# A bias row copied by another engine, and loads and scalings of q and k put elsewhere in their queues

## The chip, the core and the metric

The kernel runs on one core of a Trainium2 chip. A core has TensorE (PE in the profile, its weight loads PEld), VectorE (DVE), ScalarE (ACT), GpSimd (POOL) and SyncE (SP), which here only issues DMAs. Each engine works through its own instructions in the order in which they were written; an instruction that waits holds all that stands behind it on its engine, its DMA issues too. The metric is the device time of one execution in microseconds (us).

## What is computed

Eight batches with 12 heads of 448 tokens and 64 columns. q and k are normalized by their root mean square, attention follows, and its output, laid side by side over the heads (768 columns), goes through a gated layer whose one half is mixed over the tokens by `w_spatial`.

```python
q_n, k_n = rmsnorm(q, g_q), rmsnorm(k, g_k)      # x / sqrt(mean(x*x) + 1e-6) * g
scores = q_n @ k_n.transpose(0, 1, 3, 2) / sqrt(64)
attn = exp(scores - max); attn = attn / (sum(attn) + 1e-9)
x = (attn @ v) laid out as (batch, token, head * 64)
h = maximum(x @ w_in, 0); u, v = h[..., :512], h[..., 512:]
v_n = (v - mean(v)) / sqrt(var(v) + 1e-6)
v_s = einsum('ts,bsd->btd', w_spatial, v_n) + b_spatial[None, :, None]
out = (u * v_s) @ w_out
```

All inputs and the output are float32; the kernel multiplies in bfloat16.

## The kernel before

The 96 heads go in 24 **groups** of four heads, three groups to a batch; group 6 is the first of batch 2. For each group q and k have to be prepared: both are squared (`squares`, line 250, tile sqt; on GpSimd apart from the first ones), the squares are summed (`reduce`, line 258, tile ms, VectorE), the reciprocal root is made of the sums in two small activations (`rstd`, lines 266 and 267, tiles ln and rs, ScalarE), and q and k are multiplied by it (`scaled`, line 277, tile n; on GpSimd from group 4 on). Then a DMA issued by SyncE transposes them (`transpose_dma`, line 341, tiles qT and kr), and for k VectorE multiplies by the product of the two weight vectors (`k_scale`, line 347, tile kT). For groups 0 to 3 TensorE transposes instead.

The scores of a group are made in seven **passes** of two heads' pairs (line 367, or 363 for the pass with the odd tokens). The first 20 passes go one by one (`early`). From then on two passes make a **step**, numbered 10 to 83: eight score matmuls, then `rstd` of a group if the table puts one there, then one exponential of 128 x 1792 on ScalarE (line 374, tile et), then the rest of the table's work for this step, then either the attention output of a finished group (`attend`, lines 396 to 411: sums of the exponentials and their product with v, tile vt) or pieces of the gated layer (`fill`). Group G has its first scores at step 7G/2, rounded down.

Four things set the order of the work around the change, all written by hand. The table `todo` holds, by step, the parts of a group's preparation: `EVEN` and `ODD` give them relative to the step of the group's first scores ("sq" squares of q or k, "red" both sums, "rstd", "sc" scaling of q or k, "ks" `k_scale`), and `at` puts the transposition ("tr") one step behind each scaling. The loads of a later batch's q and k (`load_part`, four parts each, 128 rows of six heads at most; tiles qb and kb) are in the same table as "ld", from step 10 for batch 2, two parts a step. `v_step` puts the four loads of a later batch's v (`load_v`, line 130, issued by GpSimd) into steps; for batch 1 these are 10 to 13. And `load(1, 1, pool)` issues the four loads of group 1's k (lines 90 to 93, tile kf) from GpSimd at the very start.

The weights come in the first passes: `load_w_in` behind passes 3 and 8, `load_w_sp` (the spatial weights, and the bias row bst) behind pass 15, `load_w_out` at step 18. The gated layer of a batch is queued as small units (`gated`): v half (line 468), its statistics (476, 477), normalization on GpSimd (486, 490), u half (498), the mixing over the tokens (508), the output (527), its copy (443 or 445) and its store by SyncE (535 to 538). For batch 0 the queue also holds `bias_row` and four `w_sp_unit`: these bring the spatial weights, transposed by TensorE and copied by VectorE (line 223), into the tile w_spT, whose partition 64 holds the bias in its last block. The bias row is one partition of 448 values; `bias_row` writes it in three pieces, with steps of 4 or 3 elements on the reading side (lines 229 to 232).

## Time and profile before

| what | us |
|---|---|
| median of 3 runs | 344.07 |
| lowest and highest run | 343.49, 344.3 |
| profiled execution, whole | 340.97 |
| its span in the profile | 339.2 |

The profile is of one execution. Its page gives the busy time of each engine, the chain of work that ended last and the costliest groups of instructions; the trace behind it answers where an engine stood idle, for whom, and what stood in its queue then. "Idle before" is the time that an engine waited in front of an instruction, and the arrow names what ended the wait. DMA issues are shown with the engine that issues them (POOL, SPq); the time to landing is from the issue to the arrival of the data.

### The profile page before, as it was taken

The page shows a single profiled execution, that of the slowest core. Times are in us where ns is not written, and L with a number is a line of the kernel's source. Part 1 is how long each engine was busy: PE and PEld are TensorE (multiplying, and loading weights), DVE is VectorE, ACT ScalarE, POOL GpSimd, SP SyncE. Part 2 cuts the span into 40 slices and gives each one's busy share as a digit, 9 for nine tenths or more (in the row PEclk, how much of TensorE's full clock was granted, in tenths as well). Part 3 has the DMA queues.
Part 4 walks back from the last instruction along what each step waited for, and adds up shares of the span by engine and source line. Part 5 has one row for each costly group of instructions (what it writes and reads, how often), then busy time and mean ns, then how long its engine had stood idle before and what let it go on. Part 6 is the DMA issues. An engine that isn't in the chain of part 4 may idle for free.

```text
span 339.2 us, 6451 instructions
## 1 busy us (share of the span) xinstructions
PE 278.5 (82%) x2527; PEld 130.0 (38%) x2537; DVE 212.5 (63%) x343; ACT 211.2 (62%) x273; POOL 205.1 (60%) x183
## 2 busy tenths in 40 slices
PE   7587694790598799798688889779799979999994
PEld 7244331340243344244333344334334433444552
DVE  3876616499849467387467584495397486645652
ACT  2677766391157778567476778658477786675421
POOL 6759886689307499529908699359744993120210
PEclk9789978795589999989999999999799999999998
DMA  7999999829970999936992999857947387131145
GB/s 164 196 203 227 225 180 210 165 23 186 190 129 2 188 186 280 199 47 117 224 230 59 198 181 268 167 102 122 271 105 128 45 175 116 25 93 48 24 139 164
DMA packets 82944, 50.90 MB, mean 150 GB/s; under 512 B 46753, under 2 KB 79170, under 8 KB 82914
## 3 DMA queue, kind: packets, MB, share of 16 engines
q1 hardware_dynamic: 67218, 41.53, 59.1%
q0 software_dynamic: 15408, 8.73, 20.9%
q8 instruction: 20, 0.33, 0.4%
q10 hardware_dynamic: 288, 0.23, 0.2%
q14 instruction: 10, 0.08, 0.1%
HBM read 38.55 MB, written 11.01 MB: 146 GB/s over the span
## 4 chain that ended last, share of the span: by engine, by line
PE 27%; POOL 23%; DVE 15%; DMA 13%; issue 10%; ACT 6%; SPq 4%; POOLq 0%; DVEq 0%; ACTq 0%
POOL sqt L250 9%; DMA kr<-n 7%; PE ps L396 7%; POOL n L277 7%; DVE ms L258 5%; PE ps L527 4%; PE ps L508 4%; POOL vn L490 4%; PE ps L468 4%; PE ps L498 4%; ACT et L374 3%; DMA kf<-in_k_dram 3%; PE pss L367 3%; DVE s L476 3%; POOL vt L130 2%
## 5 line engine op out<-in xcount | busy, mean ns | idle before, releaser
L374 ACT ACTIVATE et<-pss 128x1792 bf16<-128x1792 f32 x74 | 122.9, 1661 | 68.5 <-PE pss L367 55.2
L411 DVE TENSOR_TENSOR xt<-ps,rc 128x448 bf16<-128x448 f32 x48 | 28.3, 621 | 62.2 <-ACT rc L404 43.5
L250 POOL TENSOR_TENSOR sqt<-kb 128x896 f32<-128x896 f32 x18 | 30.3, 1683 | 45.8 <-DVE ms L258 23.7
L367 PE MATMUL pss<-qT,kT 64*128 64x448 bf16 x254 | 38.1, 360 | 20.1 <-DVE kT L347 15.7
L396 PE MATMUL ps<-et,vt 128*32 128x448 bf16 x768 | 47.4, 385 | 7.9 <-DMA vt<-in_v_dram 5.7
L527 PE MATMUL ps<-w_out,gt 128*128 128x384 bf16 (+1 forms) x256 | 47.5, 327 | 3.0 <-DVE osb L445 2.2
L258 DVE TENSOR_REDUCE ms<-sqt 128x14 f32<-128x896 f32 x46 | 47.7, 1075 | 2.5 <-POOL sqt L250 2.5
L468 PE MATMUL ps<-w_in_v,xt 128*128 128x512 bf16 (+1 forms) x182 | 45.5, 381 | 0.4
L498 PE MATMUL ps<-xt,w_in_u 128*128 128x448 bf16 x192 | 40.3, 353 | 2.5 <-DVE osb L445 1.7
L347 DVE TENSOR_SCALAR_CACHE_REDUCE kT<-kr,g_col 128x896 bf16<-128x896 bf16 x20 | 22.7, 1136 | 26.3 <-DMA kr<-n 26.3
L396 PEld LDWEIGHTS <-vt 128*32 128x32 bf16 x768 | 23.1, 104 | 27.6 <-issue 16.2
L527 PEld LDWEIGHTS <-gt 128*128 128x128 bf16 (+1 forms) x256 | 24.2, 100 | 22.5 <-issue 9.3
L277 POOL TENSOR_TENSOR n<-qb,rs 128x896 bf16<-128x896 f32 x18 | 30.4, 1690 | 1.9 <-ACT rs L267 1.9
L367 PEld LDWEIGHTS <-kT 64*128 64x128 bf16 x276 | 10.5, 94 | 54.7 <-issue 30.9
L486 POOL TENSOR_SCALAR nm<-mv 128x4 f32<-128x4 f32 x8 | 1.8, 222 | 48.9 <-DVE mv L477 48.9
L277 POOL TENSOR_TENSOR n<-kb,rs 128x896 bf16<-128x896 f32 x18 | 30.4, 1689 | 0.1
L250 POOL TENSOR_TENSOR sqt<-qb 128x896 f32<-128x896 f32 x18 | 30.3, 1682 | 0.0
L445 DVE COPY osb<-ps 128x384 f32<-128x384 f32 (+1 forms) x45 | 24.4, 556 | 9.3 <-PE ps L527 7.9
L508 PE MATMUL ps<-w_spT,vn 128*128 128x448 bf16 (+1 forms) x128 | 28.8, 369 | 0.0
L490 POOL TENSOR_SCALAR vn<-vs,nm,rv 128x512 bf16<-128x512 bf16 (+1 forms) x32 | 24.0, 767 | 7.1 <-ACT rv L485 6.3
L498 PEld LDWEIGHTS <-w_in_u 128*128 128x128 bf16 x192 | 17.3, 98 | 21.6 <-issue 8.0
L468 PEld LDWEIGHTS <-xt 128*128 128x128 bf16 (+1 forms) x192 | 17.7, 100 | 19.8 <-issue 5.5
(94 smaller groups left out, 366.2 us busy)
## 6 DMA issues: line engine op xcount, KB each, us to landing
out_dram<-osb SPq DMA_DIRECT2D x55, 192.0 KB, 3.8
qb<-in_q_dram SPq DMA_DIRECT2D x12, 384.0 KB, 5.4
kb<-in_k_dram SPq DMA_DIRECT2D x12, 384.0 KB, 6.9
qb<-in_q_dram SPq DMA_DIRECT2D x12, 288.0 KB, 5.6
kb<-in_k_dram SPq DMA_DIRECT2D x12, 288.0 KB, 6.1
vt<-in_v_dram POOLq DMA_DIRECT2D x16, 192.0 KB, 5.1
vt<-in_v_dram POOLq DMA_DIRECT2D x16, 144.0 KB, 4.8
qf<-in_q_dram SPq DMA_DIRECT2D x10, 128.0 KB, 4.3
```

Source lines behind the costliest of these rows:

```text
L250: pool.tensor_tensor(out=t, in0=x, in1=x, op=ALU.mult)
L258: dve.tensor_reduce(out=sqs[gk][:, key[1], :], in_=sqt.pop(key).rearrange("p h c d -> p (h c) d"), axis=AX.X, op=ALU.add)
L277: (eng or pool).tensor_tensor(out=t.rearrange("p c h d -> p h c d"), in0=raw[key], in1=rst[gk][:, key[1], :].rearrange("p (h c) -> p h c", ...
L367: pe.matmul(out=ps[:, h, 0:S], lhsT=kT[r, c0:c0 + 128], rhs=qT[r, :], start=True, stop=True, tile_position=(64 * h, 0))
L374: act.activation(out=ets[s][:, 2 * a:2 * a + 2 * m, :], in_=ps[:, 0:2 * m, 0:S], func=AF.Exp, bias=0.0, scale=1.0)
L396: pe.matmul(out=ps[32 * l:32 * l + 32, 0:S], lhsT=w, rhs=et_of(G, 3 if r == 3 else r + 4 * y, h), start=(r == 0), stop=(r == 3), tile_posi ...
L411: dve.tensor_tensor(out=xts[b][:, 2 * g + half, :], in0=pst.pop((G, half))[:, 0:S], in1=rec[G], op=ALU.mult)
L468: pe.matmul(out=ps[0:m, :], lhsT=xts[b][:, j, t0:t0 + m], rhs=w_in_v[:, j, :], start=(j == 0), stop=(j == 5), tile_position=(0, 0))
L490: pool.tensor_scalar(out=vn_t[b % 2][0:m, c, :], in0=vs[b][c][0:m, :], scalar1=nms[b][0:m, c:c + 1], scalar2=rvs[b][0:m, c:c + 1], op0=ALU ...
L498: pe.matmul(out=ps[:, 0:S], lhsT=w_in_u[:, j, 128 * f:128 * f + 128], rhs=xts[b][:, j, :], start=(j == 0), stop=(j == 5))
L508: pe.matmul(out=ps[:, 0:S], lhsT=vn_t[b % 2][0:kp, c, 128 * f:128 * f + 128], rhs=w_spT[0:kp, c, :], start=(c == 0), stop=(c == NT - 1))
L527: pe.matmul(out=ps[o:o + m, 0:384], lhsT=gts[b][f][:, t0:t0 + m], rhs=w_out[:, f, r], start=(f == 0), stop=(f == 3), tile_position=(0, o))
```

## The change

The three copies of `bias_row` go from VectorE to ScalarE. The four loads of group 1's k are issued by GpSimd behind its first square and no longer ahead of it. The four loads of batch 1's v go together behind pass 15, ahead of the squares of group 4 and of the spatial weights. In the table, q of a group from 5 on is scaled in the step of its `rstd`, where it had a step of its own behind it, and k one step sooner than it was (group 5's k comes one step later); groups 6 and 7 are put one or two steps later than that, apart from `k_scale`. The loads of batch 2 begin at step 12 and not at 10.

```diff
--- before.py
+++ after.py
@@ -148,7 +148,6 @@
     g_row = const.tile([1, 2, 2, D], FP)
     pool.dma_start(out=g_row[:, 0], in_=bass.AP(tensor=g_q.tensor, offset=g_q.offset, ap=[[0, 1], [0, 2], [1, D]]))
     pool.dma_start(out=g_row[:, 1], in_=bass.AP(tensor=g_k.tensor, offset=g_k.offset, ap=[[0, 1], [0, 2], [1, D]]))
-    load(1, 1, pool)
     eps = const.tile([P, 1], FP)
     dve.memset(eps, 1e-6)
     one_f = const.tile([1, 1], FP)
@@ -226,10 +225,10 @@
         row = w_spT[64:65, NT - 1, :]
         b = bst[64:65, :]
         main = row[:, 0:384].rearrange("o (m r) -> o m r", r=P)
-        dve.tensor_copy(out=main[:, :, 0:64],
-                        in_=b[:, 0:256].rearrange("o (r m) -> o m r", m=4)[:, 0:3, :])
-        dve.tensor_copy(out=main[:, :, 64:128], in_=b[:, 256:S].rearrange("o (r m) -> o m r", m=3))
-        dve.tensor_copy(out=row[:, 384:S], in_=b[:, 3:256:4])
+        for o, i in ((main[:, :, 0:64], b[:, 0:256].rearrange("o (r m) -> o m r", m=4)[:, 0:3, :]),
+                     (main[:, :, 64:128], b[:, 256:S].rearrange("o (r m) -> o m r", m=3)),
+                     (row[:, 384:S], b[:, 3:256:4])):
+            act.activation(out=o, in_=i, func=AF.Copy, bias=0.0, scale=1.0)
 
 
     sqt, sqs, rst, nrm, qkt = {}, {}, {}, {}, {}
@@ -584,6 +583,7 @@
 
     squares(0, 0, 0, eng=act)
     squares(0, 1, 0)
+    load(1, 1, pool)
     reduce(0, 0, 0)
     reduce(0, 1, 0)
     squares(0, 0, 1, eng=act)
@@ -644,6 +644,7 @@
             rstd(3)
             scaled(3, 1)
             scaled(3, 0, eng=dve)
+            load_v(1, range(4))
             squares(4, 0)
             squares(4, 1)
             load_w_sp()
@@ -668,12 +669,14 @@
 
 
 
-    EVEN = {-8: ("sq", 0), -7: ("sq", 1), -6: ("red",), -5: ("rstd",), -4: ("sc", 0), -3: ("sc", 1), -1: ("ks",)}
-    ODD = {-6: ("sq", 0), -5: ("sq", 1), -4: ("red",), -3: ("rstd",), -2: ("sc", 0), -1: ("sc", 1), 2: ("ks",)}
+    EVEN = {-8: ("sq", 0), -7: ("sq", 1), -6: ("red",), -5: ("rstd",), -4: ("sc", 1), -1: ("ks",)}
+    ODD = {-6: ("sq", 0), -5: ("sq", 1), -4: ("red",), -3: ("rstd",), -2: ("sc", 1), 2: ("ks",)}
     todo = {}
 
     def at(s, G, *what):
         todo.setdefault(s, []).append((G,) + what)
+        if what[0] == "rstd" and G > 4:
+            at(s, G, "sc", 0)
         if what[0] == "sc":
             at(s + 1, G, "tr", what[1])
 
@@ -686,14 +689,13 @@
     at(12, 5, "sq", 1)
     at(13, 5, "red")
     at(14, 5, "rstd")
-    at(14, 5, "sc", 0)
-    at(14, 5, "sc", 1)
+    at(15, 5, "sc", 1)
     at(16, 5, "ks")
     for G in range(6, NGT):
         for o, what in (ODD if G % 2 else EVEN).items():
-            at(7 * (G // 2) + o, G, *what)
+            at(7 * (G // 2) + o + (2 if G < 8 and o < (-4, -2)[G % 2] else 1 if G < 8 and o < -1 else 0), G, *what)
     for b in range(2, B):
-        s0 = max(S0 if b == 2 else 17, NCH * NG * b // 2 - 17)
+        s0 = max(S0 + 2 if b == 2 else 17, NCH * NG * b // 2 - 17)
         for n in range(8):
             at(s0 + n // (2 if b < 4 else 1), NG * b, "ld", n)
 
@@ -721,7 +723,7 @@
         return (NCH * G + NCH - 1) // 2 + 1
 
     gate_step = {attend_step(NG * b + 2) + 1: b for b in range(B - 1)}
-    v_step = {10 + i: (1, [i]) for i in range(4)}
+    v_step = {}
     for s, b in gate_step.items():
         if b + 2 < B:
             v_step.update({s + 4 + i: (b + 2, [i]) for i in range(4)})
```

TensorE's instructions stand in the same order as before. Line numbers of the changed kernel are one lower from line 152 to 585. The three copies stand on ScalarE between the exponential of step 17 and the reciprocal root of group 6.

GpSimd around groups 6 and 7. Before, from the square of group 6's k on (sqt<-kb, then the squares of group 7; vn: normalizations of the gated layer of batch 0; n_1082 and n_1128 scale group 6):

```order
L250 TENSOR_TENSOR sqt<-kb 128x896
L250 TENSOR_TENSOR sqt<-qb 128x896
L250 TENSOR_TENSOR sqt<-kb 128x896
L130 DMA vt_105<-in_v_dram 64x6x256
L486 TENSOR_SCALAR nm<-mv_178 128x4
L490 TENSOR_SCALAR vn_176<-vs_866,nm,rv 128x512
L490 TENSOR_SCALAR vn_176<-vs_867,nm,rv 128x512
L490 TENSOR_SCALAR vn_176<-vs_868,nm,rv 128x512
L490 TENSOR_SCALAR vn_176<-vs_869,nm,rv 64x512
L277 TENSOR_TENSOR n_1082<-qb,rs_1035 128x2x7x64
L130 DMA vt_105<-in_v_dram 64x6x192
L277 TENSOR_TENSOR n_1128<-kb,rs_1035 128x2x7x64
```

In the change, from the square of group 6's q on (n_1115 and n_1117 scale group 6):

```order
L249 TENSOR_TENSOR sqt<-qb 128x896
L249 TENSOR_TENSOR sqt<-kb 128x896
L130 DMA vt_105<-in_v_dram 64x6x256
L485 TENSOR_SCALAR nm<-mv_173 128x4
L489 TENSOR_SCALAR vn_171<-vs_862,nm,rv 128x512
L489 TENSOR_SCALAR vn_171<-vs_863,nm,rv 128x512
L489 TENSOR_SCALAR vn_171<-vs_864,nm,rv 128x512
L489 TENSOR_SCALAR vn_171<-vs_865,nm,rv 64x512
L249 TENSOR_TENSOR sqt<-qb 128x896
L130 DMA vt_105<-in_v_dram 64x6x192
L276 TENSOR_TENSOR n_1115<-qb,rs_1110 128x2x7x64
L276 TENSOR_TENSOR n_1117<-kb,rs_1110 128x2x7x64
```

One square of group 7 has gone behind the normalizations and the other behind the scaling of group 6, both scalings of group 6 follow each other, and the squares of group 6 stand directly ahead of the normalizations.

SyncE around the loads of batch 2. Before (n_781 and n_783: group 4, n_928 and n_930: group 5; qb, kb: loads; the four q loads stand ahead of these rows):

```order
L341 DMA_TRANSPOSE qT<-n_781 128x7x128
L341 DMA_TRANSPOSE kr<-n_783 128x7x128
L105 DMA kb<-in_k_dram 64x6x256
L105 DMA kb<-in_k_dram 64x6x192
L105 DMA kb<-in_k_dram 64x6x256
L105 DMA kb<-in_k_dram 64x6x192
L341 DMA_TRANSPOSE qT<-n_928 128x7x128
L341 DMA_TRANSPOSE kr<-n_930 128x7x128
```

In the change (n_921: group 5's q):

```order
L105 DMA qb<-in_q_dram 64x6x256
L105 DMA qb<-in_q_dram 64x6x192
L105 DMA kb<-in_k_dram 64x6x256
L105 DMA kb<-in_k_dram 64x6x192
L340 DMA_TRANSPOSE qT<-n_921 128x7x128
L105 DMA kb<-in_k_dram 64x6x256
L105 DMA kb<-in_k_dram 64x6x192
L340 DMA_TRANSPOSE kr<-n_994 128x7x128
```

The q loads of batch 2 have come behind group 4's transpositions, and the last two k loads behind the transposition of group 5's q.

SyncE around the first store of the output. Before (n_1250: group 7, n_1406 and n_1464: group 8, n_1536: group 9):

```order
L341 DMA_TRANSPOSE kr<-n_1250 128x7x128
L538 DMA out_dram<-osb 64x768
L341 DMA_TRANSPOSE qT<-n_1406 128x7x128
L105 DMA qb<-in_q_dram 64x6x256
L341 DMA_TRANSPOSE kr<-n_1464 128x7x128
L105 DMA qb<-in_q_dram 64x6x192
L341 DMA_TRANSPOSE qT<-n_1536 128x7x128
```

In the change (n_1246 and n_1248: group 7, n_1383 and n_1410: group 8, n_1468: group 9):

```order
L340 DMA_TRANSPOSE qT<-n_1246 128x7x128
L340 DMA_TRANSPOSE kr<-n_1248 128x7x128
L340 DMA_TRANSPOSE qT<-n_1383 128x7x128
L537 DMA out_dram<-osb 64x768
L340 DMA_TRANSPOSE kr<-n_1410 128x7x128
L105 DMA qb<-in_q_dram 64x6x256
L340 DMA_TRANSPOSE qT<-n_1468 128x7x128
```

The transposition of group 8's q has gone ahead of the store, and that of its k right behind it, ahead of the load.

## Rows read from the trace of the kernel before

**Rows 1.** The page's line of busy time: us, share of span, instructions, per engine

```profile
PE 278.5 (82%) x2527; PEld 130.0 (38%) x2537; DVE 212.5 (63%) x343; ACT 211.2 (62%) x273; POOL 205.1 (60%) x183
```

**Rows 2.** Timeline, 72 to 92 us: start, us, engine, line, operation [idle before, releaser]

```profile
72.72 13.55 DVE L229 CAST w_spT<-bst 1x192 bf16<-1x192 f32 x1
...
86.03 1.72 POOL L250 TENSOR_TENSOR sqt<-qb 128x896 f32<-128x896 f32 x1
...
86.20 1.72 DVE L231 CAST w_spT<-bst 1x192 bf16<-1x192 f32 x1
...
91.94 1.67 ACT L374 ACTIVATE et<-pss 128x1792 bf16<-128x1792 f32 x1 [14.28 <-PE pss L367]
```

**Rows 3.** Timeline, 53 to 62 us, GpSimd and TensorE

```profile
53.01 0.70 POOL L130 DMA_DIRECT2D vt<-in_v_dram  x1
...
61.18 3.17 PE L396 MATMUL ps<-et,vt 128*32 128x448 bf16 x30 [5.68 <-DMA vt<-in_v_dram]
```

**Rows 4.** Waits of TensorE behind 91 us: total us, times, longest

```profile
PE pss L367 <- DVE kT L347: 15.1, 9, 2.6
```

**Rows 5.** ScalarE's groups by form: xcount, busy us, mean ns, idle before

```profile
L443 ACT ACTIVATE osb<-ps 128x384 f32<-128x384 f32 x16 | 7.8, 486 | 7.6 <-PE ps L527 7.4
...
L267 ACT ACTIVATE rs<-ln 128x28 f32<-128x28 f32 x23 | 5.2, 226 | 1.5
```

**Rows 6.** The page's groups: xcount, busy us, mean ns, idle before

```profile
L347 DVE TENSOR_SCALAR_CACHE_REDUCE kT<-kr,g_col 128x896 bf16<-128x896 bf16 x20 | 22.7, 1136 | 26.3 <-DMA kr<-n 26.3
...
L277 POOL TENSOR_TENSOR n<-kb,rs 128x896 bf16<-128x896 f32 x18 | 30.4, 1689 | 0.1
...
L490 POOL TENSOR_SCALAR vn<-vs,nm,rv 128x512 bf16<-128x512 bf16 (+1 forms) x32 | 24.0, 767 | 7.1 <-ACT rv L485 6.3
```

**Rows 7.** K loads of batch 2 on SyncE, 47 to 53 us: ns min/median/max, landing

```profile
L105 SPq DMA_DIRECT2D kb<-in_k_dram x4: 609/624/1749, 48.0 to 51.2; - x4
...
DMA to landing us min/median/max: 6.6/8.3/9.5
```

**Rows 8.** Timeline of SyncE's queue: issues at groups 5, 8 and 12

```profile
57.99 1.23 SPq L341 DMA_TRANSPOSE qT<-n  x1
...
109.50 0.54 SPq L538 DMA_DIRECT2D out_dram<-osb  x1
...
112.35 1.48 SPq L341 DMA_TRANSPOSE kr<-n  x1
...
160.72 1.27 SPq L341 DMA_TRANSPOSE kr<-n  x1
```

**Rows 9.** All transpositions of line 341: from issue to landing

```profile
DMA to landing us min/median/max: 2.9/5.0/14.8
```

**Rows 10.** Timeline of TensorE: scores at groups 6, 8, 11, 12 and 17

```profile
95.38 0.55 PE L367 MATMUL pss<-qT,kT 64*128 64x448 bf16 x4
...
119.16 0.55 PE L367 MATMUL pss<-qT,kT 64*128 64x448 bf16 x4 [2.25 <-DVE kT L347]
...
154.00 0.36 PE L367 MATMUL pss<-qT,kT 64*128 64x448 bf16 x2 [0.87 <-DVE kT L347]
...
168.41 0.55 PE L367 MATMUL pss<-qT,kT 64*128 64x448 bf16 x4 [2.65 <-DVE kT L347]
...
227.15 0.36 PE L367 MATMUL pss<-qT,kT 64*128 64x448 bf16 x2 [1.53 <-DVE kT L347]
```

**Rows 11.** Waits of GpSimd: total us, times, longest

```profile
POOL sqt L250 <- DMA kb<-in_k_dram: 14.7, 4, 8.5
...
POOL n L277 <- ACT rs L267: 7.5, 6, 2.6
```

**Rows 12.** Timeline, first 20 us, GpSimd and VectorE

```profile
7.39 1.04 POOL L250 TENSOR_TENSOR s<-fx 128x512 f32<-128x512 f32 x1 [2.19 <-DMA fx<-in_k_dram]
...
15.95 2.07 DVE L258 TENSOR_REDUCE ms<-sqt 128x14 f32<-128x896 f32 x2
```

**Rows 13.** GpSimd's four k loads of group 1: from issue to landing

```profile
DMA to landing us min/median/max: 3.7/3.9/4.4
```


## The prediction

> **What bounds the kernel now.** I read the page's line of busy time first [rows 1]: TensorE is the fullest engine, at 278.5 us of a span of 339.2, and the three others stand near 60%. No engine is full, so what counts is where TensorE or ScalarE stand still, and for whom. The timeline shows three kinds of such places. The first is one hole: ScalarE waits 14.28 us for scores before its exponential at 91.94, because VectorE spends 13.55 us on a cast of one partition by 192 elements, the first copy of the bias row, and all that stands behind it on VectorE waits. The second cast, of the same shape, takes 1.72 us and ends (87.92) where a square on GpSimd ends (87.75) [rows 2]. So size is not the reason: the cast waits for GpSimd. The second place is from 55.5 to 61.18, where TensorE waits 5.68 us for v of batch 1 [rows 3]. The third kind repeats: behind 91 us TensorE waits nine times, 15.1 us in all, for a k that VectorE has scaled late [rows 4].
>
> **The bias row.** Three VectorE casts go, three ScalarE copies of the same elements come. No ScalarE copy this small is in the trace; the nearest rows are 0.23 us for 28 elements and 0.49 for 384 [rows 5], so three cost 0.7 to 1.5 us. I take 1.0, since 192 lies between. They stand ahead of two small activations for group 6 and the exponential of step 18, on an engine that is 62% busy [rows 1], and delay these by 1.0 at most. What they free is the 14.28 us.
>
> How far GpSimd can hold VectorE is the question on which a page speaks. The row shows 13.55 us, eight times the longest GpSimd instruction beside it, 1.72 [rows 2]. The Trainium skill's page "SBUF — State Buffer", section "Who interferes with whom", states that VectorE and GpSimd share a port pair under an exclusive lock, that the second to issue is blocked until the first finishes, and that ScalarE never waits there. By that rule alone three casts would lose 5.2 us at most, the rest of the hole would have another cause and stay, and the sum below would end near 331; the trace differs, since one cast lost several instructions' worth, and the sum goes by the row.
>
> **v of batch 1.** Its four issues leave steps 10 to 13 and go ahead of the squares of group 4. The last is at 53.01 now [rows 3]. Five squares and two scalings of 1.7 us each [rows 2, 6] stand between its new place and its old one, so it goes out some 12 us sooner, near 41. Even the latest landing of the neighbouring loads, 9.5 us [rows 7], is then over before 55.5, and the 5.68 us go. In front of whom the issues now stand: 4 x 0.70 = 2.8 us ahead of the squares of group 4 and the spatial weights. The latter are wanted no sooner than about the bias row [rows 2]; group 4 can be 0 to 2.8 late, which the chain below hides, since it is led by a later load.
>
> **What is late next.** Both gains lie ahead of group 6, the first group of batch 2, so I follow that one. Its loads start two steps later, and in SyncE's queue the last two of its four k loads now stand behind group 5's transposition of q, which waits for GpSimd and goes out at 57.99, for 1.23 us [rows 8]. With 0.62 for each of two loads [rows 7] the last one is out at 60.5. These loads took 6.6 to 9.5 us to land [rows 7]; I take 6.6, because v is no longer on the way beside them: 67.1. Behind it stand on GpSimd a square, an issue of v, four normalizations, a square, an issue and the scaling of q and of k: 1.7 + 0.7 + 4 x 0.77 + 1.7 + 0.7 + 2 x 1.69 = 11.2 us [rows 2, 3, 6], to 78.3. A transposition lands 2.9 to 14.8 us after its issue, 5.0 in the middle [rows 9]: 83.3. VectorE scales k in 1.14 [rows 6], and TensorE starts the first scores of group 6, at step 21, near 84.5. They start at 95.38 now [rows 10]. So of 14.28 + 5.68 = 19.96 us only 10.9 stay: group 6 takes the rest back, as a new wait at step 21. Group 7, three steps on, meets w_out and the k loads of batch 3; I take 0.9 off for that: **10.0**. Ends: with the latest landings at both places (9.5 and 14.8) step 21 starts at 97.2, 1.8 us later than now; if nothing of the chain is late, all 19.96 stay.
>
> **k and q scaled one step sooner.** Of the nine waits two, 0.87 and 1.53, come with VectorE's queue late and k long landed; seven, 15.1 - 2.4 = 12.7 us, stand behind transpositions [rows 4, 10]. I worked two out. Group 8: SyncE is held by an output store until 109.50, then issues q's transposition and a load, and k's at 112.35 [rows 8]. In the change q's stands ahead of the store and k's right behind it, near 110.1: 2.2 us sooner, of a wait of 2.25 [rows 10]. Group 12: k's goes out at 160.72 [rows 8], when GpSimd has scaled it; in the change q's scaling goes into GpSimd's idle time ahead of the normalizations and an issue of v goes behind, so k is ready 1.69 + 0.70 = 2.4 us sooner, of a wait of 2.65. The five others are of these two kinds. At most 12.7 us go; since a wait that goes uncovers the next (the exponential, a VectorE copy), I take **8.0**, and keep 0 and 12.7 as ends. One cost is inside: the scaling of q waits for ScalarE's reciprocal root, and a square now stands behind it. Such waits of GpSimd are 7.5 us now, six times, at most 2.6 [rows 11].
>
> **The start.** The first square of k moves ahead of the four issues for group 1. GpSimd waits 2.19 us there for its data [rows 12], so its queue wins nothing; fewer bytes under way could at most take that wait away. Group 1's k then goes out until 8.43 + 2.8 = 11.2 and lands 3.9 us later [rows 12, 13]; its square ends at 16.8, and the second of the two reductions, which begins about 17.0 now [rows 12], hides it. With the 9.5 us from above it would be 5.4 late. I take 0, with ends at 2.2 won and 5.4 lost; the lower is likelier than the upper by far, since the loads around it are of the same size as now.
>
> **The sum.** The profiled execution took 340.97 us, 1.8 more than its span. 340.97 - 10.0 - 8.0 = 323.0. The median of the runs shown, 344.07, is 3.1 above that execution; the same 18 us off the median give **326 us**.
>
> **Rivals.** *All of it stays.* Group 6's chain is hidden, because its loads land sooner than I think: 20 + 8 go, 316 us. For it, v is out of the way of batch 2's loads; against it, the 11.2 us of GpSimd work in a row. 0.08.
>
> *Transpositions crowd.* Those of groups 6 and 7 go out among w_out and batch 3's k loads and land near the 14.8 us of [rows 9] instead of 5.0. One such landing takes most of the front's gain: 10 becomes 2, and 334 us result. For it, that landing came with the same loads under way. The Trainium skill's page "DMA: Bandwidth & Descriptors", section "Issuing engines are not separate DMA queues", has DMAs of all issuers run on the same 16 engines and interleave; by that rule the traffic decides, not the queue, and the spread of 2.9 to 14.8 agrees. 0.18.
>
> *The copy is as slow on ScalarE.* If strided reading of one partition were slow by itself, ScalarE would be blocked some 15 us in VectorE's place; the 8 us and some 2 of the front stay: 334. Against it, the same shape took 1.72. 0.03.
>
> *Slower.* GpSimd, ahead of each even group's last square, waits for ScalarE's reciprocal root; VectorE's reduction of that square, ScalarE's next root and the exponential behind it follow late. Eight even groups, 8 to 22, have this. It decides from 18.0 / 8 = 2.3 us each; at the longest such wait of the trace, 2.6 [rows 11], they lose 20.8 us, 2.8 more than is won: 347. For it, the order on GpSimd is fixed; against it, GpSimd stands idle at these places anyway, up to 8.5 us for k loads [rows 11]. 0.04.
>
> *Nothing measurable.* Gains meet a loss of their size: 344. 0.01.
>
> **How the numbers follow.** The forecast has 0.66, the rivals what stands with them. 326 is the forecast's time. A front between 3 and 15 and a steady part between 6 and 11 give 335 and 318; that holds most of the forecast and the two cases at 334, a little over 8 in 10. The measurement tells 0.2%, 0.7 us, from no change. Faster: 0.66 + 0.08 + 0.18 + 0.03 = 0.95; same 0.01; slower 0.04.
>
> **What would show it.** Right: no instruction of the bias row over 0.6 us; no wait for v at step 14; in place of the hole a shorter wait for group 6's scaled k, with its first scores near 85; TensorE's waits for scaled k behind step 28 down to some 5 us. Wrong: copies on ScalarE that last microseconds; GpSimd's waits for the reciprocal root above 15 us; group 1 late, so that all starts late; transpositions of groups 6 and 7 that land after 10 us or more.

## The result: 335.04 us, half of the gain that was forecast

The changed kernel takes 335.04 us (median of 3 runs, 334.81 to 335.10), the kernel before 344.07 (343.49 to 344.30). The ratio is 0.974, with a 95% interval from 0.972 to 0.976: 9.0 us less, where 18 were forecast (326, range 318 to 335). The profiled execution after took 335.10 us, like its median, with a span of 333.2. Two of the edited kernels below had one execution far out (1292.06 us in experiment 2, 651.83 in experiment 8); the medians given for them are those of their three others.

The page's line of busy time of the changed kernel, beside [rows 1]:

```profile
PE 281.5 (84%) x2537; PEld 131.0 (39%) x2537; DVE 200.3 (60%) x340; ACT 212.5 (64%) x276; POOL 205.3 (62%) x183
```

VectorE lost 12 us of busy time: the held casts of [rows 2] are gone, and 3.5 us of another hold, below, have come. The other engines do the same work as before, apart from ScalarE's three copies (the ten more matmuls of TensorE are records that the trace of before lacks).

The front, from the timeline of the changed kernel (start, us, engine, line, operation, [idle before, releaser]). These lines answer to [rows 2, 3, 10]:

```profile
57.40 0.93 PE L395 MATMUL ps<-et,vt 128*32 128x448 bf16 x16
...
72.42 0.56 PE L366 MATMUL pss<-qT,kT 64*128 64x448 bf16 x2 [6.64 <-DVE kT L346]
...
75.14 1.08 ACT L231 ACTIVATE w_spT<-bst 1x192 bf16<-1x192 f32 x3
...
87.35 0.55 PE L366 MATMUL pss<-qT,kT 64*128 64x448 bf16 x4
...
100.52 0.39 PE L366 MATMUL pss<-qT,kT 64*128 64x448 bf16 x2 [4.11 <-DVE kT L346]
```

The three copies take 1.08 us together. The wait of 5.68 us for v is gone (57.40). Two new waits have come: 6.64 us for group 5's scaled k at step 17, and 4.11 us for group 7's at step 24. Group 6's first scores start at 87.35; the forecast had 84.5. There TensorE does not wait for scaled k.

Behind step 28, from the waits by releaser (total us, times, longest) of the changed kernel behind 113 us. The second line answers to [rows 4], the fourth to [rows 11]:

```profile
PE ps L395 <- DVE osb L444: 7.0, 2, 3.5
PE pss L366 <- DVE kT L346: 5.6, 4, 2.1
PE ps L395 <- DVE gt L511: 2.7, 3, 1.3
...
POOL n L276 <- ACT rs L266: 17.1, 9, 4.3
```

TensorE's waits for scaled k fell from 15.1 to 5.6 us, just as forecast ("down to some 5 us"). In their place TensorE now waits 9.7 us for a copy of the output and a product of the gated layer that VectorE makes late (first and third line). The exponential of step 28 starts 5.8 us sooner than before, that of step 83, the last, 5.9: by these two traces all that the scaling won behind step 28 was given back. The trace of before is of an execution 3.1 us below the median, though, and the ratios further down leave some 3 us to this part.

The start, from the timeline of the changed kernel, VectorE and GpSimd, 17 to 22 us:

```profile
17.33 4.55 DVE L276 TENSOR_TENSOR n<-qf,rs 128x896 bf16<-128x896 f32 x1 [0.80 <-ACT rs L266]
21.81 1.08 DVE L276 TENSOR_TENSOR n<-kf,rs 128x896 bf16<-128x896 f32 x1
...
17.56 1.74 POOL L249 TENSOR_TENSOR sqt<-qf 128x896 f32<-128x896 f32 x1
19.20 1.73 POOL L249 TENSOR_TENSOR sqt<-kf 128x896 f32<-128x896 f32 x1
```

VectorE's scaling of group 1's q takes 4.55 us, its neighbour of the same shape 1.08. The exponential of step 10 starts at 44.46; before it started at 41.20. So three things are to be explained: a start that lost 3 us, a front that won less, and a steady part (the steps behind 28) that won little.

### The profile page after: what moved, and what is told of

It is laid out like the page before. It is cut to its first block, busy times and chain, and to the rows that moved or that the text cites. A ratio compares the mean times of both kernels' runs of the same rounds, so it can differ in the third digit from the quotient of the medians.

```text
span 333.2 us, 6464 instructions
## 1 busy us (share of the span) xinstructions
PE 281.5 (84%) x2537; PEld 131.0 (39%) x2537; DVE 200.3 (60%) x340; ACT 212.5 (64%) x276; POOL 205.3 (62%) x183
## 4 chain that ended last, share of the span: by engine, by line
PE 32%; POOL 21%; DMA 18%; DVE 10%; issue 8%; ACT 7%; SPq 4%; POOLq 0%; DVEq 0%; ACTq 0%
POOL sqt L249 10%; DMA kb<-in_k_dram 10%; PE ps L395 8%; PE ps L526 6%; DMA kr<-n 5%; POOL n L276 5%; PE ps L467 4%; PE ps L507 4%; ACT et L373 4%; PE ps L497 3%; PE pss L366 3%; POOL vt L130 3%; DVE ms L257 3%; POOL vn L489 3%; DMA qb<-in_q_dram 2%
## 5 line engine op out<-in xcount | busy, mean ns | idle before, releaser
L366 PE MATMUL pss<-qT,kT 64*128 64x448 bf16 x254 | 38.9, 363 | 20.5 <-DVE kT L346 16.3
L395 PE MATMUL ps<-et,vt 128*32 128x448 bf16 x768 | 45.1, 374 | 8.6 <-DVE osb L444 7.0
L526 PE MATMUL ps<-w_out,gt 128*128 128x384 bf16 (+1 forms) x256 | 48.5, 333 | 0.3 <-DVE gt L511 0.3
L467 PE MATMUL ps<-w_in_v,xt 128*128 128x512 bf16 (+1 forms) x192 | 48.7, 393 | 0.0
L497 PE MATMUL ps<-xt,w_in_u 128*128 128x448 bf16 x192 | 43.0, 369 | 1.2 <-ACT vs L436 0.7
L395 PEld LDWEIGHTS <-vt 128*32 128x32 bf16 x768 | 23.2, 101 | 25.7 <-issue 11.7
L507 PE MATMUL ps<-w_spT,vn 128*128 128x448 bf16 (+1 forms) x128 | 27.2, 353 | 2.3 <-DVE w_spT L222 2.3
```

The lines of the kernel that those rows point to most:

```text
L366: pe.matmul(out=ps[:, h, 0:S], lhsT=kT[r, c0:c0 + 128], rhs=qT[r, :], start=True, stop=True, tile_position=(64 * h, 0))
L395: pe.matmul(out=ps[32 * l:32 * l + 32, 0:S], lhsT=w, rhs=et_of(G, 3 if r == 3 else r + 4 * y, h), start=(r == 0), stop=(r == 3), tile_posi ...
L467: pe.matmul(out=ps[0:m, :], lhsT=xts[b][:, j, t0:t0 + m], rhs=w_in_v[:, j, :], start=(j == 0), stop=(j == 5), tile_position=(0, 0))
L497: pe.matmul(out=ps[:, 0:S], lhsT=w_in_u[:, j, 128 * f:128 * f + 128], rhs=xts[b][:, j, :], start=(j == 0), stop=(j == 5))
L507: pe.matmul(out=ps[:, 0:S], lhsT=vn_t[b % 2][0:kp, c, 128 * f:128 * f + 128], rhs=w_spT[0:kp, c, :], start=(c == 0), stop=(c == NT - 1))
L526: pe.matmul(out=ps[o:o + m, 0:384], lhsT=gts[b][f][:, t0:t0 + m], rhs=w_out[:, f, r], start=(f == 0), stop=(f == 3), tile_position=(0, o))
```

## The experiments

Times are medians; ratios are to the kernel before, run on the same chip, with 95% intervals. The runs of the kernel before reached from 339.35 to 348.06 us, so most intervals are 0.4 to 0.9% to either side.

**1. The bias row alone.** On the kernel before, only the three copies:

```diff
-        dve.tensor_copy(out=..., in_=...)      # three times
+            act.activation(out=o, in_=i, func=AF.Copy, bias=0.0, scale=1.0)
```

> The kernel before, with only the three copies of the bias row on ScalarE. Theory A (the hole is VectorE's cast being held by GpSimd, and most of the whole change's 9.0 us comes from this one edit): no instruction of the bias row over 0.6 us, no wait of 14 us ahead of an exponential, and 344.1 falls by 6 to 11 us, to 333 to 338. Theory B (the hole only covers a chain of group 6 that ends nearly as late, as the forecast let 9 of 20 us be covered): the wait moves to the scores of group 6 and 344.1 falls by less than 4.

344.27 us, ratio 1.002 (0.997 to 1.006): nothing was won that could be measured. Theory B holds. The exponential of step 20 came 11.1 us sooner (80.83 for 91.94), that of step 21 0.8. From the timeline of this run:

```profile
79.58 1.36 SPq L341 DMA_TRANSPOSE kr<-n  x1
...
79.86 0.81 POOL L209 DMA_DIRECT2D w_out<-in_moe_w_out_dram  x1
...
83.32 11.20 SPq L341 DMA_TRANSPOSE qT<-n  x1
...
92.97 1.15 DVE L347 TENSOR_SCALAR_CACHE_REDUCE kT<-kr,g_col 128x896 bf16<-128x896 bf16 x1 [12.26 <-DMA kr<-n]
...
94.19 0.93 PE L367 MATMUL pss<-qT,kT 64*128 64x448 bf16 x4 [11.39 <-DVE kT L347]
```

Group 6's transposition of k is issued at 79.58 and not usable before 92.97, 13.4 us later; w_out's load goes out 0.3 us behind it, and the next transposition takes SyncE 11.20 us to issue. The same places in the kernel before:

```profile
77.67 1.51 SPq L341 DMA_TRANSPOSE kr<-n  x1
...
90.90 1.13 DVE L347 TENSOR_SCALAR_CACHE_REDUCE kT<-kr,g_col 128x896 bf16<-128x896 bf16 x1
```

The busy share of the DMA engines in 40 slices from 56 to 98 us, first of this run, then of the kernel before, then of the changed kernel:

```profile
DMA  9999997798000690000006999999999999999999
```

```profile
DMA  9999995995004900000499999999999999995999
```

```profile
DMA  9999999997999999999993687596699999999999
```

In the kernel with the copies alone the engines stand nearly idle from 66 to 78 us, apart from a burst near 70, and then everything wants them at once. In the kernel before that was hardly different (66 to 76 us): group 6's k went out at 77.67 and landed 10.7 us later, at 88.39, 2.1 us behind the end of VectorE's first cast (86.27). The hole and the landing lay over much of the same time, and with the hole gone the landing, 4.6 us later still, holds the scores.

**2. w_out three steps later**, with the bias row on ScalarE, and without:

```diff
-        if s == 18:
+        if s == 21:
             load_w_out()
```

> The kernel before with the bias row copied by ScalarE (alone: 344.3 beside 343.4) and the load of w_out three steps later, at step 21. Theory N (there the hole's place was taken by group 6's transposition of k, which landed 13 us after its issue at 79.6, because w_out, v and the q loads of batch 3 went out around it; the w_out load is the largest of them): it lands within 7 us, the exponential of step 21 starts near 88 and not at 95, and the time falls by 4 to 7, to 337 to 340. Theory O (the other loads fill the DMA engines just as well): step 21 stays above 93 and the time at 342 to 345.

> The kernel before with only the load of w_out three steps later; the casts stay on VectorE. Theory N with the hole as the second cover (VectorE's cast is held by GpSimd until 86 whatever the transposition does): no change, 342 to 345. If GpSimd's row of work ends sooner here, as in the changed kernel with the casts back, where the cast was held for 6.7 us and cost nothing: 338 to 341.

339.32 us, 0.989 (0.983 to 0.995), with the copies on ScalarE; 340.10, 0.989 (0.982 to 0.995), with the casts left on VectorE (its traced execution is the one far out, so only the times are read). With the copies theory N holds: group 6's k goes out at 77.77 and is scaled at 87.67, 9.9 us later instead of 13.4 (not the 7 expected), and step 21 starts at 89.85. With the casts the first expectation failed: the hole was to cover the landing whatever w_out does, and no change was expected. The time fell as much as with the copies, as in the second case that I had named (GpSimd's row of work ends sooner), but no trace shows whether that row did. So a load put elsewhere was worth some 4 us in either kernel, the copies added nothing to it, and that the hole by itself would have held the scores as long as the landing is not shown.

**3. The casts back, in the changed kernel** (with the start as before):

```diff
-            act.activation(out=o, in_=i, func=AF.Copy, bias=0.0, scale=1.0)      # in the loop over the three pieces
+        dve.tensor_copy(out=..., in_=...)      # three times
```

> The changed kernel with the old start, and the bias row cast by VectorE again. Copying on ScalarE alone won nothing on the kernel before. Theory L (it won nothing there because group 6's transposition of k was as late, behind the loads; in the changed kernel group 6 is early, and the hole would count): one cast lasts over 8 us, the exponential of step 20 is late by 6 us or more, and the time rises by 6 to 12, to 338 to 344. Theory M (the edit is worth nothing here either, the schedule of groups 5 to 7 did it all): 331 to 333.5.

331.34 us, 0.965 (0.956 to 0.974), beside 0.969 (0.963 to 0.975) without this edit: no loss. Theory M holds. From the timeline, VectorE and GpSimd:

```profile
74.68 6.70 DVE L229 CAST w_spT<-bst 1x192 bf16<-1x192 f32 x1
...
79.51 1.68 POOL L250 TENSOR_TENSOR sqt<-kb 128x896 f32<-128x896 f32 x1
81.13 0.69 POOL L130 DMA_DIRECT2D vt<-in_v_dram  x1
81.31 0.29 DVE L231 CAST w_spT<-bst 1x192 bf16<-1x192 f32 x1
```

The cast is held again, for 6.70 us, until GpSimd's row of tensor operations ends at 81.19, over an issue of 0.72 us (75.47) inside that row; the second cast, with GpSimd issuing, takes 0.29. Step 20 is 3.6 us later for it, step 24 only 0.9, and step 28 is no later at all: the wait of 2.69 us for group 7's k that the kernel with the copies has at step 24 is absent here.

**4. The bias row on VectorE in another form**, in the changed kernel:

```diff
-            act.activation(out=o, in_=i, func=AF.Copy, bias=0.0, scale=1.0)
+            tot = st_pool.tile([P, 1], FP, name="tot")
+            dve.tensor_scalar(out=o, in0=i, scalar1=1.0, scalar2=None, op0=ALU.mult,
+                              op1=ALU.add, accum_out=tot[64:65])
```

> The changed kernel with the bias row back on VectorE, not as a cast but as a multiplication by one that also sums, the form in which this kernel scales k. Theory F (GpSimd holds VectorE only in some forms, the cast and the product of two tensors among them): each of the three lasts under 0.6 us, no hole, 335.0 within 1 us. Theory G (VectorE is held or slow on this row in any form): one of them lasts many us again, and the time rises to 340 to 346.

334.96 us, 0.974 (0.967 to 0.980), as with ScalarE. Theory F holds. The same elements, while GpSimd squares:

```profile
77.53 1.67 POOL L251 TENSOR_TENSOR sqt<-qb 128x896 f32<-128x896 f32 x1
...
78.34 0.49 DVE L232 TENSOR_SCALAR_CACHE_REDUCE w_spT<-bst 1x192 bf16<-1x192 f32 x1
```

0.49 us for what a cast took 13.55 us over [rows 2]. So it is neither the one partition nor the strides; it is the form of the instruction.

**5. v as before**, in the changed kernel with the start as before:

```diff
-            load_v(1, range(4))                # behind pass 15
 ...
-    v_step = {}
+    v_step = {10 + i: (1, [i]) for i in range(4)}
```

> The changed kernel with the old start, and v of batch 1 loaded in steps 10 to 13 again. Forecast (v's wait of 5.7 us is taken off by the early load and nothing of it is covered before group 6): a wait of 4 to 6 us for v at step 14 is back and the time rises by 4 to 6, to 336 to 338. Theory K (around steps 10 to 20 the DMA engines are full, and what v gains, the k of group 5 loses at step 17): the wait for v is back, the one at step 17 (some 6.6 us) shrinks by about as much, and the time stays within 2 us of 332.0.

333.00 us, 0.973 (0.965 to 0.980), beside 332.02, 0.969 (0.963 to 0.975). Theory K holds: by the medians the time stays within 1 us. In its trace step 15 comes 9.5 us later, since the wait for v is back (7.67 us), and group 5's wait at step 17, 7.1 us, is gone; at step 17 the two kernels are 2.8 us apart, at step 28 0.5.

**6. Group 5's k one step sooner**, on the changed kernel with the start as before and the sooner loads of experiment 9:

```diff
-    at(15, 5, "sc", 1)
+    at(14, 5, "sc", 1)
```

> The changed kernel with the old start and the sooner loads of batches 4 to 7 (323.4), and the k of group 5 scaled at step 14 and not 15, so that its transposition stands ahead of the last two k loads of batch 2 in SyncE's queue and not behind. Theory P (TensorE's new wait of 6.8 us for group 5 at step 17 comes from that order): the wait falls under 3 us, and 323.4 falls by 2 to 4, unless group 6 takes it back, whose k loads go out 2 us later. Theory Q (the DMA engines are full from 45 to 78 us, so that whichever goes first the other is late): the wait at step 17 shrinks, one at step 20 or 21 grows as much, 322.4 to 324.4.

324.59 us beside 323.42, ratios 0.944 (0.939 to 0.949) and 0.944 (0.937 to 0.951): the same. The scores of step 17, first with the edit, then without:

```profile
66.24 0.56 PE L367 MATMUL pss<-qT,kT 64*128 64x448 bf16 x2 [3.53 <-DVE kT L347]
```

```profile
69.52 0.55 PE L367 MATMUL pss<-qT,kT 64*128 64x448 bf16 x2 [6.78 <-DVE kT L347]
```

The wait shrinks by 3.3 us as wanted, step 17 starts 3.3 us sooner, and step 20 starts 2.2 us later, since group 6's last k loads have gone behind. Theory Q holds.

**7. The start as before**, in the changed kernel:

```diff
+    load(1, 1, pool)                           # ahead of dve.memset(eps, ...)
 ...
-    load(1, 1, pool)                           # behind squares(0, 1, 0)
```

> The changed kernel with the four loads of group 1's k issued at their old place at the start. Theory D (the move costs 3.3 us, since it lets two squares of group 2 run on GpSimd beside VectorE's scaling of group 1's q, which is held until they are over): that scaling lasts 1.1 us and not 4.55, the exponential of step 10 starts near 41.2 and not at 44.46, and the time falls from 335.0 by 2 to 3.3, to 331.7 to 333. Theory E (the start doesn't matter, since the loads of batch 2 set when groups 5 and 6 are ready): 334.3 to 335.7.

332.02 us, 0.969 (0.963 to 0.975): 3.0 us less by the medians, 1.7 by the ratios. The scaling of group 1's q is back at 1.09 us, step 10 starts at 40.96, and the 3.5 us won there become 3.0 at the end.

**8. What holds the start.** Three edits of the changed kernel with its new start. First w_in's loads ahead of group 2's squares; then the same with the squares written two passes later (and the sooner loads of experiment 9); then with the squares on ScalarE, which is shown:

```diff
-            squares(2, 0)
-            squares(2, 1)
             load_w_in(1)
+        elif p == 4:                           # one pass later
+            squares(2, 0, eng=act)
+            squares(2, 1, eng=act)
```

> The changed kernel, start included, but GpSimd issues the four loads of the first half of w_in ahead of the two squares of group 2 and not behind them. Theory D (GpSimd's squares hold VectorE's scaling of group 1's q for 3.5 us): GpSimd only issues while that scaling runs, it lasts 1.1 us, the exponential of step 10 starts near 41, and the time falls by 3, to 331.5 to 333. Theory J (the start is late since group 1's k or group 2's q lands late, as the 9.5 us of the forecast's bound had it): no change of more than 0.7, 334.3 to 335.7.

> The changed kernel, its start included, with the loads of batches 4 to 7 one step sooner, and with the two squares of group 2 two passes later on GpSimd (w_in's loads are issued in their place). Theory D, second form (any row of GpSimd work, not just these squares, holds VectorE's scalings of group 1; the weights ahead of the squares only moved the hold to the scaling of k, 5.75 us): with GpSimd idle there both scalings last 1.1 us, the exponential of step 10 starts at 39 to 41.5, and the time is that of the kernel with the old start and the sooner loads, 323.4, or up to 2 less: 321 to 324. Theory J (late landings, not the hold, cost the 3 us): step 10 near 44.5, 326 to 327.5.

> The changed kernel, its start included, with the two squares of group 2 on ScalarE, one pass later, so that GpSimd only issues w_in's loads while VectorE scales group 1. Theory D (GpSimd's squares hold VectorE): both scalings last 1.1 us, the exponentials behind come 2 to 4 us sooner than in the changed kernel (pass 7 at 25.2 there), step 10 starts at 40 to 42 instead of 44.5, and the time is 331.5 to 333 beside 335.0. Theory D2 (GpSimd's DMA issues hold VectorE as its squares do): one scaling still lasts 2 us or more, and half of that is won. Theory J (late landings): both scalings 1.1 us, but step 10 stays above 44, 334 to 336.

The first gave 333.94 us, 0.977 (0.968 to 0.986), and theory D seemed to fall. Its timeline shows why not:

```profile
17.41 1.09 DVE L276 TENSOR_TENSOR n<-qf,rs 128x896 bf16<-128x896 f32 x1 [0.80 <-ACT rs L266]
...
18.42 5.75 DVE L276 TENSOR_TENSOR n<-kf,rs 128x896 bf16<-128x896 f32 x1
...
19.82 1.76 POOL L249 TENSOR_TENSOR sqt<-qf 128x896 f32<-128x896 f32 x1
...
21.46 1.75 POOL L249 TENSOR_TENSOR sqt<-kf 128x896 f32<-128x896 f32 x1
```

The scaling of q is free, and the scaling of k is held instead, 5.75 us. The second (325.56 us, 0.945, 0.937 to 0.953) was no test: GpSimd waits for nothing in between, so its order came out as in the first, and k's scaling took 5.71. The third gave 330.90 us, 0.969 (0.962 to 0.976), with both scalings at 1.09 us, step 10 at 40.69, and w_in's issues on GpSimd still beside them:

```profile
17.18 1.09 DVE L276 TENSOR_TENSOR n<-qf,rs 128x896 bf16<-128x896 f32 x1 [0.80 <-ACT rs L266]
...
17.54 2.32 POOL L198 DMA_DIRECT2D w_in_v<-in_moe_w_in_dram  x4
...
18.19 1.09 DVE L276 TENSOR_TENSOR n<-kf,rs 128x896 bf16<-128x896 f32 x1
```

Theory D holds, D2 and J do not: GpSimd's squares hold VectorE's product, its DMA issues don't, and with the hold gone the new start is as good as the old one. Sooner issues of w_in are not the reason: in the first edit they go out as soon (17.56 for 17.54), and step 10 starts at 46.00. One thing stays open: in the first edit the scaling of k starts 1.4 us ahead of the square's recorded start and needs 1.1, and still was held, though GpSimd only issued until then.

**9. Scaling and loads, a square of four.** The sooner scaling alone on the kernel before (of the groups from 8 on), and the loads of batches 4 to 7 one step sooner alone on the kernel before:

```diff
-        s0 = max(S0 if b == 2 else 17, NCH * NG * b // 2 - 17)
+        s0 = max(S0 if b == 2 else 17, NCH * NG * b // 2 - (18 if b > 3 else 17))
```

> The kernel before, with only q and k of the groups from 8 on scaled as in the change. Forecast (steady term 8.0): TensorE's waits for scaled k behind 91 us fall from 15.1 us by about 9, and the time by 8, to 336. Theory C (what these waits lose, others win): the waits for scaled k fall by about 9 just the same, but GpSimd's waits for the reciprocal root rise above 15 us, waits of TensorE for a bank that VectorE empties late come in, and the time stays within 2.5 us of 344.1.

> The kernel before with only the loads of batches 4 to 7 one step sooner. Theory R (the waits for scaled k stand behind each other with the waits for loads; either alone uncovers the other): 341 to 344 beside 343.5. Theory S (the loads alone give most): 336 to 339.

339.88 us, 0.989 (0.984 to 0.994), and 338.60, 0.989 (0.985 to 0.993): each is worth some 3.8 us. For the scaling that is half of the forecast's 8: the waits that theory C named are there (16.7 us of GpSimd for the reciprocal root, 7.2 of TensorE for the copy of the output, behind 111 us), but they take back less than it said. For the loads it is more than theory R allowed alone; theory S holds. Then both on the changed kernel with the start as before: the sooner loads; the sooner loads with the old scaling; the old loads with the old scaling (old scaling: of the groups from 8 on).

> The changed kernel with the old start, and the loads of q and k of batches 4 to 7 one step sooner. Theory H (behind step 28 the change wins little because the last k load of a batch lands too late: at steps 46 and 67 GpSimd's square, VectorE's sum, ScalarE's root and the exponential wait for it in a row, and VectorE's copy of the output behind them holds TensorE 3.5 us): GpSimd's waits for k loads behind 100 us fall from 11.5 us to under 3, TensorE's two waits of 3.5 us for that copy fall under 1, and 332.0 falls by 3 to 6, to 326 to 329. Theory I (a sooner load only stands in front of a transposition in SyncE's queue, or waits there for the buffer that GpSimd still reads): 331 to 334.

> The changed kernel with the old start and the sooner loads (323.4), with q and k of the groups from 8 on scaled as before the change. Theory R (the scaling is worth the 8 us forecast for it as soon as the loads are out of the way): 329 to 332, TensorE's waits for scaled k behind 110 us up from 5.5 to over 12. Theory S (most of what was won behind step 28 is the loads'; the scaling is worth 2 to 4 at any time): 325.5 to 327.5.

> The changed kernel with the old start and with the groups from 8 on scaled as before the change; what is left of the change is its front: bias row, v, the loads of batch 2 and the steps of groups 5 to 7. If the scaling alone is worth 4 here too, 335 to 337, and the front 7 us of 343.5; if the scaling is worth its 8 here, 339 to 341, and the front 3 to 4.

| changed front, start as before | loads as in the change | loads one step sooner |
|---|---|---|
| scaling as before | 336.83, 0.978 (0.974 to 0.983) | 331.08, 0.969 (0.963 to 0.975) |
| scaling as in the change | 332.02, 0.969 (0.963 to 0.975) | 323.42, 0.944 (0.937 to 0.951) |

By the ratios either alone is worth 3.3 us of 344, and both together 11.7. The four intervals leave some 4 us either way open in that surplus of 5. In the four traces the stretch from step 28 to step 83 takes 190.3 us as before, 186.4 with the scaling, 185.6 with the loads and 179.4 with both: 3.9 and 4.7 alone, 10.9 together, a surplus of 2. So the scaling is worth 6 to 8 us as soon as the loads are out of its way; this is the forecast's term, under a condition that it did not have. Theory R holds here in the time (329 to 332 with the old scaling), and nearly in the waits for scaled k (11.1 us, over 12 expected). Where the loads stood in the way, step 46 of the changed kernel shows:

```profile
172.59 1.68 POOL L249 TENSOR_TENSOR sqt<-kb 128x896 f32<-128x896 f32 x1 [3.76 <-DMA kb<-in_k_dram]
...
174.31 1.09 DVE L257 TENSOR_REDUCE ms<-sqt 128x14 f32<-128x896 f32 x1 [2.51 <-POOL sqt L249]
...
175.43 0.32 ACT L265 ACTIVATE ln<-ms,eps 128x28 f32<-128x28 f32 x1 [3.40 <-DVE ms L257]
...
175.91 1.65 ACT L373 ACTIVATE et<-pss 128x1792 bf16<-128x1792 f32 x1
...
176.24 0.56 DVE L444 COPY osb<-ps 64x384 f32<-64x384 f32 x1
...
176.85 0.67 PE L395 MATMUL ps<-et,vt 128*32 128x448 bf16 x4 [3.45 <-DVE osb L444]
```

and the same place in the kernel before:

```profile
178.73 1.68 POOL L250 TENSOR_TENSOR sqt<-kb 128x896 f32<-128x896 f32 x1 [8.45 <-DMA kb<-in_k_dram]
...
181.71 0.32 ACT L266 ACTIVATE ln<-ms,eps 128x28 f32<-128x28 f32 x1 [0.80 <-DVE ms L258]
182.20 1.65 ACT L374 ACTIVATE et<-pss 128x1792 bf16<-128x1792 f32 x1
```

The last k load of batch 5 goes out at 164.10 in the changed kernel, lands 8.4 us later, and square, sum, root and exponential follow in a row; VectorE's copy of an output stands behind the sum, and TensorE waits 3.45 us for the buffer that it empties. From the start of that square to the exponential of step 46 it is 3.5 us before and 3.3 after. So the exponential follows the landing in both kernels. Before, the step ahead of it came so late that ScalarE waited only 0.80 us for the sum, where it now waits 3.40: step 45 starts 8.9 us sooner than before (169.87 for 178.76), step 46 only 6.3. The longest wait of [rows 11], 8.5 us, was just this load, and I had called it idle time. Waits by releaser behind 111 us, in the order of the table (scaling and loads as before; scaling; loads; both):

```profile
POOL sqt L250 <- DMA kb<-in_k_dram: 21.9, 4, 9.2
...
PE pss L367 <- DVE kT L347: 14.6, 8, 3.3
...
PE ps L396 <- DVE osb L445: 1.6, 2, 0.8
```

```profile
POOL sqt L250 <- DMA kb<-in_k_dram: 11.5, 3, 4.3
...
PE ps L396 <- DVE osb L445: 7.2, 2, 3.8
...
PE pss L367 <- DVE kT L347: 4.6, 5, 1.5
```

```profile
PE pss L367 <- DVE kT L347: 11.1, 7, 2.7
...
POOL sqt L250 <- DMA kb<-in_k_dram: 4.8, 1, 4.8
```

```profile
POOL n L277 <- ACT rs L267: 23.1, 9, 7.3
...
PE pss L367 <- DVE kT L347: 5.5, 4, 1.9
...
POOL sqt L250 <- DMA kb<-in_k_dram: 3.8, 2, 2.6
...
PE ps L396 <- DVE osb L445: 1.5, 2, 0.8
```

With the scaling alone the copy's wait replaces that for scaled k; with the loads alone most of the wait for scaled k stays; only with both do both shrink (5.5 and 1.5 us). Theory H holds in its mechanism and gave 8.6 us where 3 to 6 were expected. The waits for loads did not quite fall under the 3 us expected (3.8).

**10. What beats both kernels.** w_out at step 22, on the kernel with both; then that with the squares of group 2 on ScalarE, which lets the change's own start stand:

> The changed kernel with the old start and the sooner loads (323.4), and w_out loaded at step 22 and not 18. Theory N (w_out beside the transpositions makes them land late; here those of group 7, for which TensorE waits 3.6 us at step 24): that wait falls under 2 us and the time by 1 to 3, to 320.5 to 322.5. Theory Q (the other loads of batch 3 fill the DMA engines anyway): 322.7 to 324.5.

> The changed kernel, start included, with the squares of group 2 on ScalarE, the loads of batches 4 to 7 one step sooner and w_out at step 22. If the three gains stand in different places (start, behind step 41, group 7) they add up: some 0.7 us less than 321.6, since the start here was 0.7 sooner than the old one: 319.5 to 322.

321.61 us, 0.942 (0.937 to 0.948), and 320.94, 0.930 (0.926 to 0.934). The wait for group 7 at step 24, 3.60 us in the kernel with both, is gone in the first, and step 24 starts 2.5 us sooner; theory N holds there too. In the second, step 10 starts 1.6 us sooner than in the first, but step 24 only 0.5 and step 80 0.4: what the start wins the front takes back. The two ratios lie further apart than that, since the kernel before ran higher beside the second (344.42 us) than beside the first (341.96). The second is the fastest of all that ran, 14 us below the changed kernel.

## Why the prediction was wrong, step by step

Put on the ratios, the change adds up like this: its front 7.4 us (1 - 0.978 of 344, experiment 9; 5.8 to 9.0 by the interval), the scaling behind it 3.3 (2.7 us either way), the start 1.7 lost by the ratios (3.0 by the medians): 9.0 in all. The forecast had 10.0, 8.0 and 0.

**The steady term, 8.0, is the one that failed most: 3.3.** The working for groups 8 and 12 was right as far as it went: TensorE's waits for scaled k fell by 9.5 of the 12.7 us that they could. Wrong was the size in the step "since a wait that goes uncovers the next": it names the copy on VectorE that took over, but the 8.0 is a third taken off by feel. What makes that copy late was in the rows: GpSimd's longest wait for a k load, 8.5 us [rows 11]. I used this row only to say that GpSimd stands idle there, and did not ask what the square behind it is wanted for, and how soon behind the landing. The exponential came 3.3 us behind the start of that square, and experiment 9 shows that the load was the next bound: with the loads one step sooner the same scaling is worth 6 to 8 us.

**The start, 0, lost 1.7 to 3.0.** Both bounds were drawn for landings. Group 1's k did land 3.8 us after its issue, as taken, the first exponentials even came 2.1 us sooner, the upper end. But the moved square left GpSimd two more squares to do in one row, just when VectorE scales group 1, and the product was held for 3.5 us. The step that failed is "hides it": the reduction that follows was hidden, the scaling behind that was not looked at for what GpSimd does at the time. The mechanism was known from [rows 2]; I had asked it of the cast alone. The Trainium skill's page "SBUF — State Buffer", section "Who interferes with whom", names the form too: a VectorE instruction with two inputs from SBUF contends with a GpSimd instruction that reads SBUF. The trace agrees in kind (4.55 for 1.09 us). The same section of the Trainium skill's page leaves the form that also writes out its accumulator out of those that can take the shared ports, and experiment 4 agrees (0.49 us). The trace differs in order and extent: by the page's rule the one that issues first has the ports and the other waits until it finishes, while the product recorded from 17.33 on waited for two squares that started at 17.56 and 19.20.

**The front, 10.0, came out at 7.4, for other reasons than mine.** The chain of group 6 came out near: 84.5 forecast, 85.58 with the start as before, 87.35 with the change's own. That is in part luck: in the changed kernel its last load landed in 8.3 us and not 6.6, the transposition of k in 3.0 and not 5.0, and k, scaled at 86.74, was no longer what TensorE waited for at step 21; ahead of these scores it had waited 2.27 us, at 85.15, for VectorE's copies into w_spT. But "What they free is the 14.28 us", of the bias row, was wrong: alone it won nothing, and undone in the changed kernel it cost nothing that could be measured. The hole lay over group 6's transposition, whose landing beside w_out takes 10.7 us before and 13.4 with the copies. I had that landing as the rival "transpositions crowd", for the changed kernel, and not as what already stood under the hole in the kernel before. v won about 1 us (not resolved from 0), since group 5's new wait at step 17 took its place; my chain followed group 6 alone and passed group 5 over, though two of the loads that it moves come to stand ahead of group 5's k in SyncE's queue. And group 7 gave back 4.11 us at step 24, where I had taken 0.9. w_out's place alone was worth some 3.9 us on the kernel before, and in the change its load goes out 2 us behind group 6's k instead of 0.3; that this is half of the front's 7.4 is argued. How the rest divides between the later loads of batch 2 and the later squares of groups 6 and 7 stays open; they were not tried apart.

**The rivals.** "Slower" named GpSimd's wait for the reciprocal root, and it did rise above the 15 us that I had set as its mark: 17.1 us behind step 28. That mark was wrong. With the start as before it is 16.2 us behind 111 us, and 23.1, longest 7.3, with the sooner loads, where the kernel is 8.6 us faster: GpSimd waits there with nothing wanted of it. "Transpositions crowd" came true in part at group 7: its q landed 11.0 us after its issue in the changed kernel, and with w_out put later the wait there went (experiment 10). "The copy is as slow on ScalarE" fell: 1.08 us for the three. The rule of the page on the port pair was priced wrongly: near 331 comes out only if the 5.68 us of v are left out; with them 10.9 us go there too, and the sum is 326 again.

**The sum.** The profiled execution of before, 340.97 us, was 3.1 below its median, so by the two traces the change wins 5.9 us and by the medians 9.0. I had added the 3.1 back, which puts forecast and result on the same base, the medians; it had no part in the miss.

## What to carry to other kernels

When a hole is found, look under it: take the work that comes next and ask when its last DMA lands without the hole, since two things may be late at once, and then the removal of the larger wait alone can show nothing (14.28 us here). A wait of an engine that "stands idle anyway" is free only if what follows it is not wanted soon; the distance from its end to the next exponential says so (3.3 us here). And a moved instruction has to be checked for what runs on the other engine beside its new neighbours, not only for its own data.

## What was not expected of the hardware

- VectorE's cast and its product of two tensors were held beside GpSimd's tensor operations, 4.55, 5.75, 6.70 and 13.55 us for 0.29 to 1.09 us of work, and let go when the last of a row of them ended or, before, between two squares (86.07). In the kernel before two DMA issues in a row inside GpSimd's work (77.33 to 78.75) had not let the cast go; issues alone did not hold the product (1.09 us beside 2.32 us of issues, experiment 8). Nor is it always VectorE that loses: before, its product of 25.38 took 1.09 us, and GpSimd's product that starts 0.05 us later took 2.60 for 1.69. The sum-writing multiplication was not held (0.49 us).
- A transposition of 128 x 896 landed 3.0 us after its issue where the last load had gone out 4 us before it (77.96; 82.24 to 85.24 in the changed kernel), and 13.4 us after it with a load of 768 KB and the loads of a batch around it (experiment 1); and SyncE's own issue of the next one took 11.20 us instead of 1.2, with all loads behind it.
- Two edits that were worth 3.9 and 4.7 us alone were worth 10.9 together (the four traces of experiment 9; by the ratios 3.3, 3.3 and 11.7).
